# A linear-attention and MoE kernel: one 128-partition fetch per quad of chunks, in the order chunk, batch, head

## The chip, the cores and the metric

The kernel runs on one core of a Trainium2 chip. The metric is device time in microseconds of one launch; lower is better. Three runs of the kernel before gave 773.69, 776.86 and 777.75 us, so its time is the median, 776.86 us.

## The reference

An RWKV-7 style recurrence over 768 time steps, for 4 batches and 8 heads of dimension 40, is followed by an MLP over the 3072 tokens that it gives. All data is float32.

```python
for t in range(S):                                  # S = 768; B, H, D = 4, 8, 40
    y[:, :, t] = einsum('bhd,bhde->bhe', r_t, state)
    Sa = einsum('bhde,bhe->bhd', state, a_t)
    state = state * w_t[:, :, None, :] - einsum('bhd,bhe->bhde', Sa, b_t)
    state = state + einsum('bhd,bhe->bhde', v_t, k_t)
x = y.transpose(0, 2, 1, 3).reshape(B * S, H * D)   # 3072 x 320
h = x @ w_in                                        # w_in 320 x 2048
out = (h * cos(h)) @ w_out                          # w_out 2048 x 320
```

## The kernel before

Time is cut into 24 chunks of C = 32 steps. Inside a chunk the recurrence is turned into small matrix products, with all 4 batches and 8 heads at once: 128 partitions are 4 batches times 32 steps, or 64 partitions are one head's 40 features with padding. W, the running product of the decays w inside a chunk, scales a, b, k and the state. From chunk to chunk the state is handed on by the steps `t`, `q`, `x`, `s`, `z` of a chunk (`ch_t` to `ch_z`). In `ch_z` VectorE writes `qz`, GpSimd multiplies it by W (line 910) and makes `yt` (line 921), and `tokens` (line 926, SyncE's queue) stores it. Two chunks make a group; the MLP of a group (`fa`, `fb`, `y`, `sd` or `u`, `m`, `ms`, `c`) fills TensorE between the small products.

Everything is issued in an order that is written out by hand, the string `PLAN`: 1536 tokens such as `rf:r:2`. Each token calls one function, and each engine, and each DMA queue, takes its instructions in that order. Nothing is reordered at run time; an instruction that waits holds up all behind it on its engine. `B:n`, `K:n` and `P:n` are idle matmuls that keep TensorE busy.

The operands come in two ways. For early chunks they are loaded in natural layout (`load`, token `ld`, line 267) and transposed on TensorE. From the third quad of chunks on (a, r and v from quad 2, w from quad 3; a quad is four chunks; the dictionary `SINCE`) they are transposed through DRAM:

1. `rf:n:q` calls `quad_fetch` (line 278; for w `sf:q` calls it through `ws_fetch`): it loads one quad of one input into `ws`, 128 partitions of 32 steps x 40 features, 5120 B per partition. There is one `ws`. The partitions are (chunk, head, batch), which takes four DMAs of 32 partitions (line 282), each with the heads outermost.
2. `pt:n:q:i` (`quad_turn`, line 296, GpSimd) copies a third of the features out of `ws`, transposed in the free dimension, into one of two staging tiles `nat_a`; `st` (`quad_store`, line 303) stores it to DRAM as feature, partition, step. For w, `sc` (`ws_scan`, lines 350 and 355, VectorE) first makes W in `ws`, and `ss` stores it as the tensor `wd`.
3. `lt:c:n` (`turned_load`, line 323) loads one chunk of it with the features on the partitions, in two DMAs of 40 partitions: into `aT`, `rT`, `vp` (which holds v turned) or `wb` (W turned).
4. For chunks 12 to 23 `ld:c:w` also loads W in natural layout from `wd`, in one DMA (line 259), for `over_w` (token `r`, a reciprocal on VectorE).

The fetch of one quad cannot start before the last `pt` of the quad fetched before it has read `ws`.

Of the kernel before, what the change touches and what calls it, by code (L numbers as in the profile page):

```python
# [9 lines left out]
F32 = mybir.dt.float32  # L10
I32 = mybir.dt.int32
U32 = mybir.dt.uint32
ALU = mybir.AluOpType
# [7 lines left out]
sc:1 pb:2 lo:0 pn:2 lo:2 L:0:k:s:r is:0 ip:0:15 wf:1 wt:1 ip:0:14 ip:0:13 ip:0:12 ip:0:11 ip:0:10 ip:0:9  # L21
L:0:k:s:l L:0:v:p:l kn:0 k:0 wf:0 L:1:k:p:l ld:5:a ip:0:8 ip:0:7 in:0 L:1:v:s:l B:3 v:0 g:0 L:1:k:s:r wm:1
ip:0:6 ip:0:5 L:1:r:p:l wg:1 B:4 L:1:v:p:r kn:1 k:1 ip:0:4 wp:1 L:1:r:s:r in:1 v:1 wf:2 L:2:k:p:r ip:0:3 wt:2
ip:0:2 ip:0:1 ss:1 L:2:k:p:l x:0 it:0 g:1 B:4 L:2:v:s:r L:2:r:p:r ih:0 F:0:0:0 L:2:v:s:l ld:4:w wm:2 wf:3
S:0:0:0 wf:6 wg:2 wp:2 L:2:r:s:l wt:0 wg:0 s:0 wm:0 B:4 K:6 wt:3 wm:3 K:4 wf:4 wg:3 in:2 z:0 kn:2 B:5 t:1 q:1
wf:7 wp:0 ld:5:w L:3:r:p:l B:4 wp:3 F:0:1:0 K:14 wt:4 L:3:r:p:r wt:6 wm:4 F:0:2:0 L:3:v:p:l k:2 wg:4 wp:4
S:0:1:0 wf:8 wf:9 B:5 wf:5 K:6 L:3:v:s:r wt:7 wm:7 wg:7 wm:6 L:3:k:s:r wg:6 wp:6 x:1 wt:9 B:3 B:4 wp:7 s:1
wm:9 v:2 wg:9 wt:8 wm:8 B:4 wp:9 tk:0 wg:8 g:2 B:3 wf:10 wf:12 wt:5 wp:8 L:3:k:s:l wf:11 wt:10 wm:10 B:6 z:1
B:6 t:2 q:2 wg:10 ld:4:b B:6 wm:5 wg:5 tk:1 wp:5 in:3 wt:11 wm:11 B:3 wf:13 wp:10 x:2 kn:3 k:3 wt:13 tb:0 tb:1
wg:11 wp:11 S:0:2:0 v:3 ld:4:r wt:12 wm:13 wg:13 wp:13 wm:12 K:6 ld:4:k fa:0:0 fb:0:0 y:0:0:0 wg:12 wf:14  # L30
y:0:0:1 wt:14 wm:14 y:0:0:2 K:29 wg:14 g:3 s:2 wp:12 fa:0:1 ld:4:v fb:0:1 wp:14 F:0:3:1 y:0:1:1 y:0:1:0
sd:0:0:0 wf:15 wt:15 wm:15 wf:16 z:2 y:0:1:2 in:4 r:4 sd:0:0:1 sd:0:1:1 K:13 wt:16 wm:16 wf:17 S:0:3:1 wg:15
t:3 ld:5:b r:5 pw:4 wg:16 wp:15 K:20 ld:4:a sf:2 sc:2 q:3 ld:5:r fa:0:2 fb:0:2 y:0:2:0 x:3 pb:4 wt:17 ld:6:b
wm:17 y:0:2:1 wf:18 ld:7:w y:0:2:2 wp:16 sd:0:1:0 wf:19 wt:19 wm:19 kn:4 wg:17 wp:17 sd:0:2:1 ld:6:w ld:7:b
s:3 T:0:0 wg:19 pa:4 wt:18 wp:19 ss:2 r:6 ld:5:v ld:6:a pw:6 rf:a:2 r:7 tk:2 fa:0:3 pn:4 lo:4 fb:0:3 y:0:3:0
z:3 pb:6 ld:7:a pa:6 wg:18 pn:6 lo:6 y:0:3:1 y:0:3:2 wm:18 wp:18 is:4 ld:5:k sd:0:2:0 t:4 sp:4 ip:4:15 ld:8:w
kn:5 ld:8:b k:4 v:4 ip:4:14 g:4 ip:4:13 ip:4:12 ip:4:11 sd:0:3:0 in:5 tk:3 pt:a:2:0 ip:4:10 ip:4:9 ip:4:8
ip:4:7 ld:9:w tb:2 tb:3 ip:4:6 ip:4:5 v:5 k:5 fa:1:0 ip:4:4 ip:4:3 ip:4:2 st:a:2:0 q:4 g:5 fb:1:0 y:1:0:0
pt:a:2:1 ip:4:1 st:a:2:1 pt:a:2:2 st:a:2:2 rf:r:2 pt:r:2:1 ld:6:r lt:9:a x:4 pt:r:2:0 y:1:0:1 it:4 ld:9:b
ld:6:v sd:0:3:1 F:4:0:1 y:1:0:2 sd:1:0:0 ih:4 S:4:0:1 in:6 F:4:1:1 ld:6:k r:9 r:8 s:4 ld:11:b fa:1:1 pw:8  # L40
fb:1:1 y:1:1:0 z:4 lt:8:a y:1:1:1 sd:1:0:1 S:4:1:1 sp:8 T:1:0 F:4:3:1 F:4:2:1 t:5 pb:8 xa:9 xa:8 o:0:0
st:r:2:0 pt:r:2:2 ld:11:w y:1:1:2 fa:1:2 tk:4 ld:10:w rf:v:2 q:5 r:11 ld:10:b fb:1:2 x:5 sd:1:1:1 r:10 y:1:2:0
pn:8 sd:1:1:0 st:r:2:1 y:1:2:1 lt:11:a s:5 st:r:2:2 kn:6 ld:7:k ld:7:v pt:v:2:0 tb:4 v:6 y:1:2:2 sd:1:2:1 z:5
fa:1:3 k:6 pw:10 g:6 xa:11 st:v:2:0 fb:1:3 lt:10:a y:1:3:1 pb:10 S:4:3:1 tk:5 S:4:2:1 o:0:1 sd:1:2:0 y:1:3:0
# [84 lines left out]
def kernel(  # L129
# [145 lines left out]
    def re_laid(n, q):  # L275
        return q >= SINCE[n]
# [942 lines left out]
```

## Time and profile before

| | us |
|---|---|
| median of three runs | 776.86 |
| the profiled execution | 781.72 |
| its span, first to last instruction | 780.0 |
| TensorE busy in it | 714.6 |
| VectorE, ScalarE, GpSimd busy | 548.6, 358.3, 287.3 |
| busy share of the 16 DMA engines, 0 to 145 us / 145 to 560 / 560 to 780 | 0.62 / 0.54 / 0.18 |

Names of lines in the profile are those of the listing above. `SPq` is the queue of SyncE, which issues nearly all DMAs; `POOLq` is GpSimd's. The span from about 145 to 560 us is the one in which quads are fetched and turned; ahead of it lies the opening, in which the weights and the first chunks are loaded, and behind it the end, in which nothing more is fetched by quads.

### The profile page before, as it was taken

The page shows a single profiled execution, that of the slowest core. Times are in us where ns is not written, and L with a number is a line of the kernel's source. Part 1 is how long each engine was busy: PE and PEld are TensorE (multiplying, and loading weights), DVE is VectorE, ACT ScalarE, POOL GpSimd, SP SyncE. Part 2 cuts the span into 40 slices and gives each one's busy share as a digit, 9 for nine tenths or more (in the row PEclk, how much of TensorE's full clock was granted, in tenths as well). Part 3 has the DMA queues.
Part 4 walks back from the last instruction along what each step waited for, and adds up shares of the span by engine and source line. Part 5 has one row for each costly group of instructions (what it writes and reads, how often), then busy time and mean ns, then how long its engine had stood idle before and what let it go on. Part 6 is the DMA issues. An engine that isn't in the chain of part 4 may idle for free.

```text
span 780.0 us, 40147 instructions
## 1 busy us (share of the span) xinstructions
PE 714.6 (92%) x17948; PEld 588.9 (75%) x17948; DVE 548.6 (70%) x1199; ACT 358.3 (46%) x719; POOL 287.3 (37%) x466
## 2 busy tenths in 40 slices
PE   4758999899997989989899999899999999999996
PEld 3536678687785767878788778778888878888885
DVE  6988779887546886658878577899547886454343
ACT  1335574744544534543533544335445445445342
POOL 7624304233440562561452533542533223231111
PEclk9879999999999999999999999999999999999999
DMA  7675464554544456455446647447422231120100
GB/s 109 147 207 120 136 162 123 123 97 99 119 96 120 88 124 148 110 112 125 97 105 142 142 111 156 93 108 144 107 55 48 48 83 29 33 53 22 29 18 17
DMA packets 233405, 78.12 MB, mean 100 GB/s; under 512 B 193744, under 2 KB 224208, under 8 KB 233232
## 3 DMA queue, kind: packets, MB, share of 16 engines
q1 hardware_dynamic: 230992, 73.90, 42.4%
q8 instruction: 141, 2.31, 1.3%
q0 software_dynamic: 1152, 1.48, 1.0%
q10 hardware_dynamic: 1088, 0.16, 0.1%
q14 instruction: 32, 0.26, 0.1%
HBM read 54.53 MB, written 20.97 MB: 97 GB/s over the span
## 4 chain that ended last, share of the span: by engine, by line
PE 70%; DVE 9%; SPq 5%; DMA 5%; issue 4%; ACT 3%; POOL 2%; DVEq 0%; POOLq 0%; ACTq 0%
PE ph L210 25%; PE po L210 18%; PE dps L210 4%; PE x0ps L210 4%; PE gram L210 3%; PE sps L210 3%; PE p L210 2%; PE qps L210 2%; PE nps L210 2%; SPq L267 2%; PE sT L800 2%; DVE inv L652 1%; PE busy L210 1%; DMA xT<-xd 1%; ACT turns L995 1%
## 5 line engine op out<-in xcount | busy, mean ns | idle before, releaser
L210 PE MATMUL ph<-xT,w_in_sb 128*128 128x256 f32 x768 | 185.6, 388 | 5.3 <-DVE gT L998 2.4
L210 PEld LDWEIGHTS ph<-xT,w_in_sb 128*128 128x128 f32 x768 | 141.2, 191 | 34.0 <-issue 12.5
L210 PE MATMUL po<-w_out_sb,gT 128*128 128x160 f32 (+1 forms) x624 | 132.9, 353 | 0.9 <-DVE gT L998 0.8
L988 ACT ACTIVATE turns<-ph,few 128x512 f32<-128x512 f32 x96 | 63.6, 687 | 136.8 <-PE ph L210 134.6
L990 DVE SCALAR_TENSOR_TENSOR turns<-turns,ph 128x512 f32<-128x512 f32 x96 | 63.4, 684 | 84.8 <-ACT turns L988 84.2
L210 PEld LDWEIGHTS po<-w_out_sb,gT 128*128 128x128 f32 x624 | 99.8, 195 | 18.3 <-DVE gT L998 1.6
L910 POOL TENSOR_TENSOR qz<-qz,wc 128x160 f32<-128x160 f32 x92 | 40.2, 461 | 125.7 <-DVE qz L909 125.7
L998 DVE TENSOR_TENSOR gT<-ph,turns 128x512 f32<-128x512 f32 x96 | 65.1, 684 | 19.6 <-ACT turns L995 19.4
L296 POOL COPY nat_a<-ws 128x416 f32<-128x416 f32 (+1 forms) x45 | 46.5, 1044 | 70.0 <-DMA wdv<-nat_a 27.9
L995 ACT ACTIVATE turns<-turns,few 128x512 f32<-128x512 f32 x96 | 69.3, 722 | 3.1
L994 ACT ACTIVATE turns<-turns 128x512 f32<-128x512 f32 x96 | 59.9, 624 | 16.7 <-DVE turns L990 16.7
L1078 POOL TENSOR_TENSOR s<-gT 128x256 f32<-128x256 f32 x36 | 28.6, 795 | 82.8 <-DVE gT L1074 82.8
L652 DVE TENSOR_TENSOR inv<-inv,inv_tmp 128x31 f32<-128x31 f32 (+15 forms) x124 | 56.0, 452 | 4.3
L210 PE MATMUL ph<-xT,w_in_tail 64*128 64x256 f32 (+1 forms) x456 | 54.2, 396 | 0.0
L210 PE MATMUL po<-TW,gT 128*128 128x160 f32 x288 | 53.1, 308 | 0.1
L648 DVE TENSOR_TENSOR inv_tmp<-u,inv 128x31 f32<-128x31 f32 (+15 forms) x124 | 50.2, 405 | 2.7
L818 ACT COPY qz<-qps 40x256 f32<-40x256 f32 x92 | 33.8, 367 | 36.8 <-PE qps L210 35.4
L210 PEld LDWEIGHTS po<-TW,gT 128*128 128x128 f32 x288 | 45.1, 198 | 0.3 <-DVE gT L1074 0.3
L559 POOL TENSOR_TENSOR bn<-nat_b,rw 128x320 f32<-128x320 f32 x22 | 19.9, 908 | 67.6 <-DVE rw L558 51.7
L558 DVE RECIPROCAL rw<-nat_w 128x320 f32<-128x320 f32 x20 | 42.6, 2138 | 2.4 <-DMA nat_w<-wd 2.4
L1070 POOL TENSOR_TENSOR s<-gT 128x256 f32<-128x256 f32 x36 | 27.0, 751 | 46.6 <-DVE gT L998 29.0
L210 PEld LDWEIGHTS ph<-xT,w_in_tail 64*128 64x128 f32 (+1 forms) x456 | 32.2, 169 | 11.2 <-issue 6.6
(156 smaller groups left out, 1255.8 us busy)
## 6 DMA issues: line engine op xcount, KB each, us to landing
words<-in_moe_w_in_dram SPq DMA_DIRECT2D x8, 512.0 KB
xd<-yt SPq DMA_DIRECT2D x48, 80.0 KB
out_dram<-ot SPq DMA_DIRECT2D x24, 160.0 KB
nat_k<-in_k_dram SPq DMA_DIRECT2D x90, 40.0 KB
nat_v<-in_v_dram SPq DMA_DIRECT2D x88, 40.0 KB
nat_b<-in_b_dram SPq DMA_DIRECT2D x84, 40.0 KB
wd<-ws SPq DMA_DIRECT2D x5, 640.0 KB
xT<-xd SPq DMA_DIRECT2D x24, 128.0 KB
```

Of the source, the lines that this page charges most:

```text
L210: nc.tensor.matmul(o, lhsT=lhsT, rhs=rhs, start=start, stop=stop, skip_group_check=True)
L296: nc.gpsimd.tensor_copy(quad_part(n, q, i).rearrange("p (d t) -> p d t", t=C), ws[:, :, PARTS[i]].rearrange("p t d -> p d t"))
L558: nc.vector.reciprocal(rw, wn)
L648: nc.vector.tensor_tensor(tmp, u[:, j : j + 1, :j].to_broadcast([P, C - j, j]), x[:, j:, j : j + 1].to_broadcast([P, C - j, j]), ALU.mult,)
L652: nc.vector.tensor_tensor(x[:, j:, :j], x[:, j:, :j], tmp, ALU.subtract)
L818: nc.scalar.copy(pick(qz[rows], f * (NZ - C), (NZ, 2 * B), (1, C)), ps[f][rows, : 2 * B * C].rearrange("p (i t) -> p i t", t=C),)
L910: nc.gpsimd.tensor_tensor(z, z, wc.rearrange("p (f m b) -> p f m b", f=2, m=2)[:, :, :, bb] .unsqueeze(3).to_broadcast([P, 2, 2, D]), ALU. ...
L988: nc.scalar.activation(t, u, ACTF.Identity, bias=rnd, scale=1.0)
L990: nc.vector.scalar_tensor_tensor(t, t, -ROUND, u, ALU.add, ALU.subtract)
L994: nc.scalar.activation(t, t, ACTF.Abs)
L995: nc.scalar.activation(t, t, ACTF.Sin, bias=half_pi, scale=-2.0 * math.pi)
L998: nc.vector.tensor_tensor(gT[:, 2 * e : 2 * e + 2, :n], phs[e], ns[e].rearrange("p (f t) -> p f t", f=2), ALU.mult)
```

## The change

The partitions of `ws` become (chunk, batch, head). Batch and head lie behind one another in DRAM with one step, so one DMA of 128 partitions fetches the quad, with the chunks outermost (4 chunks, 32 pairs of batch and head, 5120 B). What follows from the new order of the partitions:

- `wd` is (chunk, batch, head, step, feature); natural W is loaded by four DMAs of 32 partitions instead of one of 128.
- In `turned_load`, r and v come back in runs of 512 B instead of 2048 B, a and W in runs of 128 B instead of 512 B.
- The turned tiles are laid out batch, head instead of head, batch. The matmuls take the same blocks of 32 columns from other places (`piece`); three elementwise operations (`turned_a`, the multiplication of `qz`, that of `yt`) walk W or their own tile in another order (`in_order`), with the same number of elements.

`PLAN` is another written order of the same steps: the tokens are the same, 1536 in number, but for the queues on which some first loads are issued (`L:chunk:input:queue:half`, queue s, a or p for SyncE, ScalarE, GpSimd, halves l and r of the four batches). The tokens from a fetch to the first that reads it (`pt`, or `sc` for w) are these:

| fetch | a2 | r2 | v2 | w3 | a3 | r3 | v3 | w4 | a4 | r4 | v4 | w5 | a5 | r5 | v5 |
|---|---|---|---|---|---|---|---|---|---|---|---|---|---|---|---|
| before | 38 | 1 | 19 | 1 | 12 | 16 | 12 | 9 | 31 | 1 | 14 | 24 | 13 | 15 | 31 |
| after | 12 | 5 | 21 | 4 | 1 | 7 | 11 | 10 | 10 | 5 | 1 | 2 | 19 | 3 | 1 |

The first lines of the written order, and the code:

```diff
@@ PLAN @@
 PLAN = """
-L:1:b:p:r L:0:a:s:l B:5 L:2:b:s:r L:1:a:p:r L:1:w:s:l L:0:v:p:r L:0:w:a:r L:0:w:s:l L:3:a:s:l B:4 L:3:b:p:l
-L:0:b:s:r L:1:w:a:r L:0:a:p:r L:2:w:s:r L:0:b:p:l L:1:a:s:l L:1:b:s:l L:2:w:s:l L:0:r:s:l L:3:b:s:r L:3:w:p:l
-L:3:w:s:r pw:0 L:2:a:s:l L:2:a:s:r L:2:b:s:l B:3 pa:0 L:0:r:p:r pw:2 L:3:a:s:r pa:2 pb:0 sp:0 pn:0 sf:1 B:2
...
+L:1:a:p:l L:2:w:s:l L:0:w:a:r L:0:b:p:r L:1:b:s:r L:0:v:p:r B:4 L:0:a:p:r B:5 B:3 L:3:w:s:r L:1:w:s:l
+L:1:w:a:r L:0:w:s:l L:3:b:p:r L:2:b:s:r L:3:w:s:l L:0:a:s:l L:0:k:s:r L:3:a:s:r L:1:a:p:r L:0:b:p:l L:2:b:s:l
+pw:0 L:2:w:s:r L:2:a:p:r L:0:r:s:r L:1:b:s:l L:2:a:p:l pa:0 L:3:b:p:l pw:2 L:3:a:s:l pa:2 sp:0 sf:1 pb:0 pn:0
+L:0:k:s:l sc:1 pb:2 pn:2 lo:2 L:0:v:s:l B:4 lo:0 kn:0 is:0 wf:1 L:0:r:s:l in:0 L:1:r:p:l L:1:k:p:r L:1:k:s:l
...
@@ -255,15 +255,10 @@
     def load(c, names, via=nc.sync, parts=range(B)):
         for n in names:
-            if n == "w" and re_laid("w", c // 4):
-                via.dma_start(
-                    nat[n, c][:, :, :D], wd[c // 4][c % 4].rearrange("h b t d -> (b t) h d")
-                )
-                continue
             for i in parts:
                 at_c = src[n][i, :, c * C : (c + 1) * C, :]
                 if n == "w" and c >= 4:
-                    at_c = wd[c // 4][c % 4, :, i] if re_laid("w", c // 4) else wd[c // 4][i, :, c % 4]
+                    at_c = wd[c // 4][c % 4, i] if re_laid("w", c // 4) else wd[c // 4][i, :, c % 4]
                 via.dma_start(nat[n, c][blk[i], :, :D], at_c.rearrange("h t d -> t h d"))
@@ -277,12 +272,11 @@
     def quad_fetch(n, q):
-        for i in range(4):
-            x = src[n]
-            nc.sync.dma_start(
-                ws[blk[i]].rearrange("p t d -> p (t d)"),
-                bass.AP(x.tensor, x.offset + (4 * q + i) * C * D, [[S * D, H], [H * S * D, B], [1, C * D]]),
-            )
+        x = src[n]
+        nc.sync.dma_start(
+            ws.rearrange("p t d -> p (t d)"),
+            bass.AP(x.tensor, x.offset + 4 * q * C * D, [[C * D, 4], [S * D, B * H], [1, C * D]]),
+        )
     PARTS = [slice(0, 14), slice(14, 27), slice(27, D)]
@@ -319,20 +313,32 @@
             G[tag, c] = aT_b[c % 6] if n == "a" else sb2.tile([P, 4, P], F32, tag=tag, name=tag)
             to = G[tag, c].rearrange("p j t -> p (j t)")
         for e in range(2):
-            x = turned_d[n, c // 4][:, 4 * H * (c % 4) : 4 * H * (c % 4 + 1)]
-            nc.sync.dma_start(
-                to[half[e]].rearrange("p (j t) -> p j t", j=4),
-                x.rearrange("d (f j b) t -> f d j (b t)" if n in "vr" else "d (j f b) t -> f d j (b t)", f=2, b=B)[e],
-            )
+            x = turned_d[n, c // 4][:, B * H * (c % 4) : B * H * (c % 4 + 1)]
+            if n in "vr":
+                at_e, x = to[half[e]].rearrange("p (b n) -> p b n", b=B), x.rearrange("d (b f j) t -> f d b (j t)", f=2, b=B)
+            else:
+                at_e, x = to[half[e]].rearrange("p (n t) -> p n t", t=C), x.rearrange("d (n f) t -> f d n t", f=2)
+            nc.sync.dma_start(at_e, x[e])
     def turned_w(c):
         wc = G["wc", c] = ring.tile([P, 4 * B], F32, tag="wc", name="wc")
         nc.gpsimd.tensor_copy(wc, G["wb", c][:, C::C])
         from_one(c)
+    def in_order(n, c, x):
+
+        form = "p (b j) t -> p j b t" if re_laid(n, c // 4) else "p (j b) t -> p j b t"
+        return x.rearrange(form, j=4)
+
+    def piece(n, c, rows, j, b):
+
+        if re_laid(n, c // 4):
+            return G[n + "T", c][rows, b, j * C : (j + 1) * C]
+        return G[n + "T", c][rows, j, blk[b]]
+
     def turned_a(c):
-        aT = G["aT", c].rearrange("p j t -> p (j t)")
-        nc.vector.tensor_tensor(b4(aT), b4(aT), G["wx", c], ALU.mult)
+        aT = in_order("a", c, b4(G["aT", c].rearrange("p j t -> p (j t)")))
+        nc.vector.tensor_tensor(aT, aT, in_order("w", c, G["wx", c]), ALU.mult)
     def ws_fetch(q, via=nc.sync):
         if re_laid("w", q):
@@ -356,7 +362,7 @@
             n //= 2
     def ws_store(q):
-        wd[q] = dram.tile([4, H, B, C, D] if re_laid("w", q) else [B, H, 4, C, D], F32, tag="wd", name="wd")
+        wd[q] = dram.tile([4, B, H, C, D] if re_laid("w", q) else [B, H, 4, C, D], F32, tag="wd", name="wd")
         nc.sync.dma_start(wd[q].rearrange("x y z t d -> (x y z) (t d)"), ws.rearrange("p t d -> p (t d)"))
     def first_load(c, name, queue, parts):
@@ -606,7 +612,7 @@
                     for e in range(2):
                         mm(
                             ps[e][blk[bb ^ e], (4 * i + j) * C : (4 * i + j + 1) * C],
-                            G["bT", c + i][half[e], j, blk[bb]], G["aT", c + i][half[e], j, blk[bb]],
+                            G["bT", c + i][half[e], j, blk[bb]], piece("a", c + i, half[e], j, bb),
                             i == 0 and j == 0,
                         )
@@ -750,21 +756,21 @@
         nc.scalar.copy(G["kT", c].rearrange("p j t -> p (j t)"), ps)
     def p2_g(c):
-        kT, vT, aT, rT = G["kT", c], G["vT", c], G["aT", c], G["rT", c]
+        kT = G["kT", c]
         ps = two("gram")
         for j in range(4):
             for bb in range(B):
                 for e in range(2):
                     mm(
                         ps[e][blk[bb], j * C : (j + 1) * C], kT[half[e], j, blk[bb]],
-                        aT[half[e], j, blk[bb]], j == 0,
+                        piece("a", c, half[e], j, bb), j == 0,
                     )
         for j in range(4):
             for bb in range(B):
                 for e in range(2):
                     mm(
-                        ps[e][blk[bb], (4 + j) * C : (5 + j) * C], vT[half[e], j, blk[bb]],
-                        rT[half[e], j, blk[bb]], False,
+                        ps[e][blk[bb], (4 + j) * C : (5 + j) * C], piece("v", c, half[e], j, bb),
+                        piece("r", c, half[e], j, bb), False,
                     )
         ag = sb2.tile([P, H, C], F32, tag="ag", name="ag")
         n = HH * C
@@ -811,7 +817,7 @@
                 for f in range(2):
                     mm(
                         ps[f][half[e], i * C : (i + 1) * C], G["s", c][half[f], i, half[e]],
-                        G["rT", c][half[f], 2 * (i % 2) + e, blk[i // 2]], i == 0,
+                        piece("r", c, half[f], 2 * (i % 2) + e, i // 2), i == 0,
                     )
         for f in range(2):
             for rows in half:
@@ -837,7 +843,7 @@
                     for e in range(2):
                         mm(
                             ps[e][blk[bb ^ e], j * N72 : (j + 1) * N72],
-                            G["aT", c][half[e], j, blk[bb]], qz[half[e], bb, j % 2, o : o + N72], False,
+                            piece("a", c, half[e], j, bb), qz[half[e], bb, j % 2, o : o + N72], False,
                         )
         x0 = [sb1.tile([P, 4 * N72], F32, tag=f"x0{e}", name=f"x0{e}") for e in range(2)]
         nc.scalar.copy(x0[0], ps[0][:, : 4 * N72])
@@ -909,7 +915,9 @@
                 nc.vector.tensor_tensor(z, pick(dp, 0, (2 * N72 + C, 2), (N72, 2), (1, D)), z, ALU.add)
                 nc.gpsimd.tensor_tensor(
                     z, z,
-                    wc.rearrange("p (f m b) -> p f m b", f=2, m=2)[:, :, :, bb]
+                    wc.rearrange(
+                        "p (b f m) -> p f m b" if re_laid("w", c // 4) else "p (f m b) -> p f m b", f=2, m=2
+                    )[:, :, :, bb]
                     .unsqueeze(3).to_broadcast([P, 2, 2, D]),
                     ALU.mult,
                 )
@@ -918,9 +926,12 @@
                 pick(dp, D, (2 * N72 - D, 2), (N72, 2), (1, C)),
                 pick(qz[:, bb], 0, (NZ - C, 2), (NZ, 2), (1, C)), ALU.add,
             )
-        nc.gpsimd.tensor_tensor(
-            yt.rearrange("p j b t -> p (j b) t"), yt.rearrange("p j b t -> p (j b) t"), wx, ALU.mult
-        )
+        if re_laid("w", c // 4):
+            nc.gpsimd.tensor_tensor(yt, yt, in_order("w", c, wx), ALU.mult)
+        else:
+            nc.gpsimd.tensor_tensor(
+                yt.rearrange("p j b t -> p (j b) t"), yt.rearrange("p j b t -> p (j b) t"), wx, ALU.mult
+            )
         G["yt", c] = yt
     def tokens(c):
```

More of the change, by code (lines that the diff above doesn't have):

```diff
@@ new lines @@
+ld:6:r F:4:2:1 t:5 fa:1:2 tk:4 lt:10:a S:4:1:1 q:5 ld:10:b fb:1:2 xa:9 in:6 y:1:2:0 ld:7:k x:5 lt:11:a
+sd:1:1:0 s:5 k:6 pt:v:2:0 r:11 sp:8 y:1:2:1 sd:1:1:1 pt:v:2:1 pn:8 y:1:2:2 sd:1:2:1 z:5 o:0:0 ld:7:v tk:5
+fa:1:3 v:6 pw:10 xa:10 st:v:2:0 pt:v:2:2 tb:4 g:6 r:10 fb:1:3 ld:7:r in:7 y:1:3:0 y:1:3:1 S:4:3:1 xa:11
+sd:1:2:0 tb:5 pb:10 S:4:2:1 y:1:3:2 o:0:1 pn:10 is:8 sf:3 t:6 ij:8:31 fa:2:0 sc:3 kn:7 k:7 q:6 v:7 ij:8:30
+st:v:2:2 fb:2:0 y:2:0:1 x:6 sd:1:3:0 sd:1:3:1 ij:8:29 ij:8:28 ij:8:27 ij:8:26 st:v:2:1 ss:3 y:2:0:0 lt:8:r
@@ new lines @@
+ld:12:b y:2:0:2 ij:8:25 ld:12:w ld:13:w s:6 pt:w:3:0 st:w:3:0 lt:8:v fa:2:1 fb:2:1 z:6 y:2:1:1 ij:8:24
+sd:2:0:0 sd:2:0:1 T:0:1 y:2:1:0 y:2:1:2 T:3:0 o:1:0 r:12 tk:6 g:7 ld:8:v ld:8:k ij:8:23 ij:8:22 t:7 fa:2:2
+ij:8:21 q:7 o:1:1 pt:w:3:2 fb:2:2 x:7 T:0:2 T:0:3 y:2:2:1 lt:9:r pt:w:3:1 st:w:3:2 ij:8:20 ij:8:19 y:2:2:0
+kn:8 y:2:2:2 sd:2:1:0 k:8 st:w:3:1 s:7 ld:9:k sd:2:1:1 ij:8:18 ij:8:17 ij:8:16 z:7 ij:8:15 ij:8:14 rf:a:3
+pt:a:3:1 pt:a:3:0 ld:13:b ld:9:v kn:9 lt:12:w fa:2:3 r:13 fb:2:3 sd:2:2:1 T:1:1 g:8 tk:7 ij:8:13 y:2:3:1
@@ new lines @@
+m:3:1:0 fa:3:2 fb:3:2 ld:14:b x:9 rf:v:3 y:3:2:0 o:2:0 lt:10:v u:3:1:2 m:3:1:1 tk:8 xa:12 T:3:1 lt:13:a
+ld:14:w pt:v:3:0 lt:11:r xa:13 u:3:1:3 y:3:2:1 sp:12 s:9 lt:14:w y:3:2:2 lt:15:a T:3:2 ld:11:k r:15 o:2:1
+u:3:2:0 pn:12 T:3:3 k:10 xw:14 fa:3:3 st:v:3:0 T:2:3 z:9 tb:8 r:14 pt:v:3:1 pt:v:3:2 fb:3:3 y:3:3:0 t:10
+lt:14:a xa:14 tk:9 m:3:2:0 u:3:2:1 y:3:3:1 u:3:2:2 g:10 y:3:3:2 lt:15:w xw:15 xa:15 m:3:2:1 u:3:2:3 pb:14
+pn:14 u:3:3:0 u:3:3:1 m:3:3:0 u:3:3:2 is:12 sf:4 ij:12:31 ij:12:30 tb:9 ij:12:29 ij:12:28 st:v:3:1 m:3:3:1
@@ new lines @@
+tk:13 fa:5:3 st:v:4:1 r:18 fb:5:3 m:5:2:0 u:5:2:2 g:14 u:5:2:3 pt:v:4:2 y:5:3:1 m:5:2:1 y:5:3:0 xa:18 pb:18
+y:5:3:2 lt:19:w t:14 xw:19 xa:19 pn:18 u:5:3:0 u:5:3:1 tb:13 is:16 sf:5 fa:6:0 sc:5 q:14 m:5:3:0 ij:16:31
+ij:16:30 ij:16:29 ld:15:v fb:6:0 x:14 pt:w:5:1 ld:15:k st:v:4:2 u:5:3:2 kn:15 k:15 y:6:0:1 m:5:3:1 u:5:3:3
+ms:5 c:5:0 y:6:0:0 ij:16:28 ss:5 c:5:1 ij:16:27 u:6:0:0 ij:16:26 ld:20:b y:6:0:2 u:6:0:1 pt:w:5:0 fa:6:1
+ld:21:b c:5:3 c:5:2 lt:15:v st:w:5:0 pt:w:5:2 s:14 ld:16:k st:w:5:1 ij:16:25 ij:16:24 fb:6:1 y:6:1:0 rf:a:5
@@ new lines @@
+z:14 m:6:0:0 u:6:0:2 t:15 y:6:1:2 y:6:1:1 ld:20:w u:6:0:3 ij:16:23 st:w:5:2 g:15 lt:16:v m:6:0:1 u:6:1:0
+ld:16:v u:6:1:1 ij:16:22 ij:16:21 pt:a:5:1 fa:6:2 q:15 o:5:0 pt:a:5:0 st:a:5:0 r:20 o:5:1 fb:6:2 y:6:2:1
+lt:17:r m:6:1:0 lt:16:r x:15 u:6:1:2 ld:21:w tk:14 ij:16:20 y:6:2:0 y:6:2:2 kn:16 ld:17:v k:16 s:15 ld:17:k
+ij:16:19 ij:16:18 ij:16:17 ij:16:16 pt:a:5:2 m:6:1:1 u:6:1:3 st:a:5:2 ij:16:15 ij:16:14 z:15 fa:6:3 fb:6:3
+y:6:3:0 u:6:2:0 u:6:2:1 m:6:2:0 u:6:2:2 ij:16:13 t:16 y:6:3:2 y:6:3:1 kn:17 g:16 m:6:2:1 ij:16:12 r:21 tb:14
@@ new lines @@
+ms:7 c:7:1 c:7:2 ij:20:31 lt:19:v st:v:5:2 s:18 o:7:0 u:8:0:0 ij:20:30 kn:19 k:19 ld:20:k ld:20:v ij:20:29
+ij:20:28 u:8:0:1 fa:8:1 ij:20:27 c:7:3 ij:20:26 ij:20:25 st:v:5:1 z:18 fb:8:1 g:19 kn:20 ij:20:24 m:8:0:0
+u:8:0:2 tk:18 ij:20:23 ij:20:22 t:19 q:19 m:8:0:1 u:8:0:3 y:8:1:1 y:8:1:0 ij:20:21 y:8:1:2 u:8:1:0 k:20 x:19
+u:8:1:1 m:8:1:0 u:8:1:2 lt:21:r lt:20:v lt:20:r ld:21:k fa:8:2 ij:20:20 u:8:1:3 ij:20:19 ij:20:18 ij:20:17
+ij:20:16 s:19 o:7:1 fb:8:2 z:19 y:8:2:0 tk:19 y:8:2:1 m:8:1:1 t:20 u:8:2:0 y:8:2:2 u:8:2:1 fa:8:3 q:20
@@ L119 @@
+u:11:2:1 fa:11:3 fb:11:3 y:11:3:0 m:11:2:0 u:11:2:2 u:11:2:3 y:11:3:1 m:11:2:1 y:11:3:2 u:11:3:0 u:11:3:1
+m:11:3:0 u:11:3:2 u:11:3:3 m:11:3:1 c:11:0 c:11:1 c:11:3 ms:11 c:11:2 o:11:0 o:11:1
 """
```

163 lines of the change are left out of this document (65 added, 98 removed).

## The prediction

> **What bounds the kernel now.** I read the page, then busy time by stage, then what each engine waited for, then the lines of `ws`. TensorE bounds it:
>
> ```profile
> PE 714.6 (92%) x17948; PEld 588.9 (75%) x17948; DVE 548.6 (70%) x1199; ACT 358.3 (46%) x719; POOL 287.3 (37%) x466
> PE 70%; DVE 9%; SPq 5%; DMA 5%; issue 4%; ACT 3%; POOL 2%; DVEq 0%; POOLq 0%; ACTq 0%
> ```
>
> The first line is busy time, the second the chain that ended last. Of 780.0 us TensorE is idle for 65. By stages its busy time is 115.8 of 145 us, 390.1 of 415 and 208.7 of 220, so 29, 25 and 11 us of idle. The fetches by quads lie in the middle stage. What TensorE waited for there (total, times, longest):
>
> ```profile
> PE gram L210 <- issue: 5.0, 4, 2.6
> PE nps L210 <- issue: 4.5, 4, 2.3
> PE sps L210 <- ACT x L843: 3.7, 1, 3.7
> PE ph L210 <- DVE gT L998: 2.4, 2, 1.8
> PE bT L514 <- DVE yt L916: 1.9, 1, 1.9
> ```
>
> About half is "issue", behind no other engine; the waits for engines that another order could take away are some 12 us, one of 3.7 the largest. So the upside is small, a few us. What happened at that largest one, and at three other fetches (in brackets the idle time ahead):
>
> ```profile
> 231.90 2.93 SPq L282 DMA_DIRECT2D ws<-in_w_dram  x4
> 239.14 1.35 DVE L350 TENSOR_TENSOR ws<-ws 128x640 f32<-128x640 f32 x2 [6.27 <-DMA ws<-in_w_dram]
> 247.02 0.31 PE L210 MATMUL sps<-x,rt 32*32 32x72 f32 x2 [3.69 <-ACT x L843]
> ...
> 180.72 1.98 POOL L296 COPY nat_a<-ws 128x416 f32<-128x416 f32 x2 [7.80 <-DMA aT<-wda]
> 301.71 1.99 POOL L296 COPY nat_a<-ws 128x416 f32<-128x416 f32 x2 [9.44 <-DMA aT<-wda]
> 422.11 1.98 POOL L296 COPY nat_a<-ws 128x448 f32<-128x448 f32 x2 [5.46 <-DMA nat_b<-in_b_dram]
> ```
>
> The fetch w3 is issued at 231.90 and read at 239.14, 7.24 us later; VectorE stands for 6.27 us and TensorE then loses 3.69. The GpSimd rows are the fetches r2, r3 and r4: each is issued 7.0 to 7.4 us before the copy begins, so it is the fetch that is waited for, whatever name stands behind the arrow. GpSimd is 37% busy and usually loses nothing by it.
>
> How fast a fetch is (us; busy of PE, PEld, DVE, ACT, POOL; clock; DMA share; GB/s):
>
> ```profile
> 118.00:120.64 2.64, 2.64 (x69) 1.99 (x52) 2.64 (x11) 1.59 (x3) 1.50 (x4) 1.00 0.82 254
> 233.42:238.58 5.16, 5.16 (x150) 4.19 (x152) 0.00 (x0) 3.81 (x8) 0.00 (x0) 1.00 0.42 133
> ...
> L282 SPq DMA_DIRECT2D ws<-in_w_dram x12: 665/686/752, 231.9 to 457.7; - x12
> L341 SPq DMA_DIRECT2D ws<-in_w_dram x2: 587/648/708, 18.1 to 116.6; - x2
> ```
>
> Both stretches hold one transfer of 655 KB in rows of 5120 B and next to nothing else. The first is L341, one DMA whose outermost count is 32; the second the four DMAs of L282, outermost count 8. The DMA time is the same, 0.82 x 16 x 2.64 = 34.6 us and 0.42 x 16 x 5.16 = 34.7, but the second has half of the engines, and takes twice as long.
>
> **The change part by part.**
>
> *SyncE's queue.* Removed: 60 issues of L282 at 0.67 us, 40.2. Added: 15 at 0.65 (L341, the nearest row), 9.8; W's natural load becomes four issues (L267, 0.45 us) instead of one (L259, 0.39) for 12 chunks, 21.6 - 4.7 = 16.9. Net -13.5 us of queue time. SPq is 5% of the chain, but mostly as waiting for producers; I take -1, between -4 and 0.
>
> *The landing of a fetch.* The new DMA has outermost count 4. Going from 32 to 8 halved the engines; the bounds are 34.7 us of DMA time over 16 engines (2.2 to 2.64 us as measured) and over 4 (8.7 us). With 1.5 us from issue to first packet (231.90 to 233.4) and 0.5 from the last packet to VectorE's start, it lands 4.6 or 10.7 us after its issue, where it was 7.24. I take 10.7, since L282 against L341 is a row for just this difference. The Trainium skill ("DMA: Bandwidth & Descriptors", in the section on why a DMA increments its semaphore by 16, paragraph "How many engines (k)") says that a DMA runs on the largest number up to 16 that divides the outermost sizes of both sides: 16, 8 and now 4. The trace agrees on 16 and 8; no run shows the 4 yet. By that rule the sum is the forecast's, by 16 engines that of the first rival below.
>
> *Who waits.* The new order puts the reader closer behind the fetch: the median distance falls from 14 tokens to 5, and distances of up to 5 tokens go from 3 of 15 to 8. Before, five fetches were waited for: 7.80, 6.27, 9.44, 5.46 and 1.77 us (v3), 30.7 in all, and TensorE lost 4.2 us at w3 (3.69 and 0.49 right behind), 1.0 at r2 (0.49 and 0.54, the latter for GpSimd's memset of `half` queued behind the copy), and nothing I can attribute at the others: 5.2 / 30.7 = 0.17 us per us waited. After: 8 close ones at 8 us (10.7 less what SyncE runs ahead) and three of 7 to 10 tokens (r3, w4, a4) at 3 us, 73 in all, 42 more. At 0.17 that is +7 us. The bounds: 0, if all are like r4 (nothing lost), and 42 x 4.2 / 6.27 = +28, if all are like w3. Queued behind a waiting `pt` on GpSimd are `qz` and `yt` of `ch_z`, `kn`, `bn` and the sums `s`; behind a waiting `sc` on VectorE the cosine's and the chain's steps. Loads issued behind the fetch stand behind it on the engines that it holds and land up to 3 us later; I count that in the same term.
>
> *Shorter runs.* `aT` and `wb` come in 56 DMAs of 640 runs instead of 160, the same bytes (80 KB). `wda<-nat_a` and its like already write runs of 128 B, so the size is nothing new here. They are prefetched; the worst waits for them now are 16.8 us of GpSimd in 5 times (`wc`), not of TensorE. I take +0.5, between 0 and 3, the four W loads included (VectorE waited 2.4 us once for one).
>
> *Elementwise walks.* The `yt` product takes 1.27 us for 128x512 (2.5 ns an element), the `qz` product, which already walks strided and broadcast operands, 0.44 us for 160 (2.7): no change of rate to be expected, 0. The matmuls keep shapes and number: 0. If the walk cost a tenth more on 12 chunks it would be 0.13 us each, on an engine with 63% idle.
>
> *The opening.* The first wait is for `a` of chunk 0:
>
> ```profile
> 9.97 1.15 POOL L267 DMA_DIRECT2D nat_a<-in_a_dram x2
> 14.44 0.63 PE L514 MATMUL aps<-ident,nat_a 128*128 128x128 f32 x4 [2.65 <-DMA nat_a<-in_a_dram]
> ```
>
> Those loads move from the fifth place on GpSimd's queue to the fourth, 1.15 us earlier; `a` of chunk 1 goes from the second to the sixth, where it lands at about 15.4, just when it is read now (15.43). VectorE's inverse of quad 0 loses one weight step (`wp:1`, 0.6 us) from ahead of it. I take -1, between -2 and +1. GpSimd now issues a2 between `pw:0` and `pa:0`, at about 14 to 16 us; read at 20.4, it is in time.
>
> *The end* is the same work in the same order on TensorE; 0. The rest of the order: 0, between -4 and +4, since the movable idle time of the middle is 12 us.
>
> The sum against the profiled execution: 781.7 - 1 + 7 + 0.5 - 1 = 787.2. The median of the runs stands 4.9 lower (776.86 to 781.72), so 782.3, +0.7%. A measurement of this kernel tells some 0.5% (3.9 us) from no change.
>
> **The rivals.**
>
> *Faster: the fetch gets all 16 engines, like L341.* It lands after 4.6 us instead of 7.24. For it: 128 partitions on the other side, as in L341. Against it: outermost count 4. Eleven waits of about 3 us are 33 us, as many as now, but w3's 3.69 us of TensorE shrinks by 2.6; with the queue's -1 to -2 and the opening's -1 that is -5: 772. It decides if a fetch takes under 5 us. The Trainium skill (same page, "Rules for kernel authors") advises 128 partitions and few large transfers; by that rule alone this rival would be the forecast. The same time comes out if the fetch is slow but SyncE issues it well ahead.
>
> *No difference.* GpSimd has 63% of its time free, and r3 and r4 cost TensorE nothing; if all the new waits are like these, 777.
>
> *Much slower.* GpSimd's waits fall ahead of `qz` in most quads, and the state's chain loses as at w3: +28 - 2, about 803.
>
> **How the numbers follow.** Forecast (781 to 795) 0.48; much slower 0.10; no difference 0.15; faster 0.27, since an order with less idle time is possible for reasons I cannot see in parts. Slower by over 0.5% is 0.58. The range 767 to 798 takes in the faster case with the order's -4 and most of the slower ones.
>
> **What would show it.** Right: in the stretch of a fetch the DMA share near 0.25 and 8 us or more of 5120 B rows; 15 issues of the fetch, near 0.65 us each; waits of `nat_a` copies on GpSimd well over the 70.0 us of now; TensorE idle in 145 to 560 us over 25. Wrong: a fetch of 2.6 us at a share near 0.8; or long fetches whose readers do not wait, because SyncE is ahead; or a difference that arises before 145 or after 560 us, where no quad is fetched.

## The result: 44 us slower, and the profile after

The kernel after takes 819.0 us (median of 4 runs, 816.0 to 826.6), the kernel before 775.3 in the same comparison: a ratio of 1.060 (95% interval 1.049 to 1.070). Slower by 5 us was forecast, in a range that ended at 798 us, and it is slower by 44. Ratios, here and below, leave out runs that lie over 1.5% above the fastest of their kernel; medians are of all runs. The profiled execution took 817.4 us, its span is 815.7. Busy time, and the chain of work that ended last:

```profile
PE 725.2 (89%) x17948; PEld 593.8 (73%) x17948; DVE 551.4 (68%) x1199; ACT 360.5 (44%) x719; POOL 289.9 (36%) x468
PE 47%; DVE 21%; DMA 12%; POOL 6%; SPq 6%; issue 4%; ACT 4%; DVEq 0%; POOLq 0%; ACTq 0%
```

TensorE's instructions are as many, but its share of the chain fell from 70% to 47%. TensorE is idle for 90.5 us (65.4 before), and the same matmuls take 10.6 us longer. So the 35.7 us by which the two profiled spans differ are 25.1 of idle time and 10.6 of busy time (they differ by less than the medians, since the profiled execution before was one of the longer ones). The stage in which quads are fetched (us, busy of PE, PEld, DVE, ACT, POOL, clock, DMA share, GB/s):

```profile
145.00:560.00 415.00, 370.52 (x9573) 302.24 (x9574) 283.54 (x610) 179.74 (x365) 160.97 (x239) 0.95 0.52 105
```

9573 matmuls ran in these 415 us, where it had been 10439, and TensorE is idle for 44 of them instead of 25. The `yt` product of chunk 3 starts 1.6 us earlier than before, that of chunk 5 8.4 later, of chunk 8 14.8, 11 21.2, 14 36.3; from there to chunk 23 it stays between 33 and 37. The loss arises where quads are fetched, and nowhere else. What TensorE waited for there (total, times, longest):

```profile
PE nps L210 <- DVE aT L341: 8.5, 2, 5.2
PE bT L520 <- POOL bn L565: 6.3, 2, 4.4
PE kT L520 <- POOL kn L740: 5.3, 2, 2.8
...
PE ph L210 <- DMA xT<-xd: 2.8, 1, 2.8
```

No large wait carries it: there are some twenty waits of at most 5.2 us, spread over all operands. The fetch itself, from what uses `ws` (least/median/longest issue in ns; then who waited for `ws`, in us and times):

```profile
L276 SPq DMA_DIRECT2D ws<-in_w_dram x3: 582/606/917, 238.0 to 491.2; - x3
...
  POOL nat_a L290: 70.8, 8
  DVE ws L356: 12.4, 3
```

Each fetch is one issue of about 0.6 us, as predicted. GpSimd's copies waited for `ws` eight times, 70.8 us in all: six times for a fetch (43.0 us) and twice for VectorE's scan of w (27.7 us). The fetch w3, which opened the prediction, in the timeline (idle time ahead in brackets):

```profile
238.04 0.58 SPq L276 DMA_DIRECT2D ws<-in_w_dram  x1
249.80 2.22 DVE L356 TENSOR_TENSOR ws<-ws 128x640 f32<-128x640 f32 x5 [6.62 <-DMA ws<-in_w_dram]
253.87 1.05 POOL L290 COPY nat_a<-ws 128x448 f32<-128x448 f32 x1 [14.95 <-DVE ws L361]
```

From issue to reader it is 11.8 us now, where it was 7.24. Rows of 5120 B stand in the trace for 7.4 to 10.7 us per fetch. Where the fetch has the engines to itself, they are busy to 0.26, about 4 of 16 (clock, DMA share and GB/s at the end):

```profile
246.00:247.00 1.00, 1.00 (x8) 0.92 (x7) 0.00 (x0) 0.94 (x4) 0.00 (x0) 1.00 0.26 108
```

At r2, r3, r4 and a5 the copy waited for one thing more. It writes a staging tile whose last store is issued 0.7 to 3.0 us behind the fetch, and by the trace's semaphores that store landed 1.0 to 1.7 us after the fetch did. At r2:

```profile
181.02 0.99 POOL L290 COPY nat_a<-ws 128x416 f32<-128x416 f32 x1 [11.44 <-DMA wda<-nat_a]
```

What the prediction had not looked for is in SyncE's queue. Behind a fetch the *issues* themselves last long. A fetch of r, and one of v, with what is issued behind:

```profile
169.61 0.60 SPq L276 DMA_DIRECT2D ws<-in_r_dram  x1
170.25 6.38 SPq L297 DMA_DIRECT2D wda<-nat_a  x2
...
205.36 0.58 SPq L276 DMA_DIRECT2D ws<-in_v_dram  x1
...
206.50 11.88 SPq L262 DMA_DIRECT2D nat_r<-in_r_dram  x4
```

Two issues take 6.38 us and four take 11.88, where one has a median of 0.45. All issues of three kinds (least/median/longest, ns):

```profile
L297 SPq DMA_DIRECT2D wda<-nat_a x12: 382/471/5860, 165.1 to 552.0; - x12
L262 SPq DMA_DIRECT2D nat_v<-in_v_dram x88: 311/450/8304, 17.9 to 718.4; - x88
L942 SPq DMA_DIRECT2D xd<-yt x48: 273/358/4932, 78.5 to 762.1; - x48
```

The medians are nearly those of before (491, 450 and 357 ns), but the longest had been 1324, 2222 and 955. I call *held* what SyncE's rows of issues in 140 to 640 us last beyond 0.55 us per issue, summed over the rows in which it is over 1.5 us: 26 us before, 102 after. One such case through to TensorE:

```profile
332.76 0.60 SPq L276 DMA_DIRECT2D ws<-in_v_dram  x1
339.23 5.21 SPq L321 DMA_DIRECT2D aT<-wda  x2
343.12 1.05 POOL L290 COPY nat_a<-ws 128x448 f32<-128x448 f32 x1 [6.01 <-DMA ws<-in_v_dram]
347.16 0.69 DVE L341 TENSOR_TENSOR aT<-aT,wb 128x512 f32<-128x512 f32 x1 [4.23 <-DMA aT<-wda]
347.91 0.76 PE L210 MATMUL nps<-aT,bT 40*32 40x32 f32 x64 [3.22 <-DVE aT L341]
```

The second load of `aT` is held in its issue until 344.4, VectorE waits 4.23 us for it, TensorE 3.22 for VectorE; no reader of `ws` stands between them. And then the clock (last column but two):

```profile
344.00:348.00 4.00, 0.78 (x81) 0.67 (x86) 0.84 (x2) 0.32 (x2) 2.83 (x6) 1.00 0.41 77
348.00:352.00 4.00, 3.76 (x74) 3.20 (x75) 3.51 (x5) 1.84 (x4) 0.41 (x1) 0.57 0.71 129
```

After those 3.22 us the granted clock is 0.57 for the next four, which is another 0.43 x 3.76 = 1.6 us lost, by this estimate. The longer busy time fits that: the mean clock of the middle stage fell from 0.98 to 0.95, and 0.03 x 370.5 is 11 us.

### The profile page after: what moved, and what is told of

It is laid out like the page before. It is cut to its first block, busy times and chain, and to the rows that moved or that the text cites. A ratio compares the mean times of both kernels' runs of the same rounds, so it can differ in the third digit from the quotient of the medians.

```text
span 815.7 us, 40129 instructions
## 1 busy us (share of the span) xinstructions
PE 725.2 (89%) x17948; PEld 593.8 (73%) x17948; DVE 551.4 (68%) x1199; ACT 360.5 (44%) x719; POOL 289.9 (36%) x468
## 4 chain that ended last, share of the span: by engine, by line
PE 47%; DVE 21%; DMA 12%; POOL 6%; SPq 6%; issue 4%; ACT 4%; DVEq 0%; POOLq 0%; ACTq 0%
PE ph L210 16%; PE po L210 11%; DVE inv L658 4%; DVE inv_tmp L654 3%; DMA ws<-in_a_dram 3%; PE x0ps L210 3%; DMA ws<-in_w_dram 3%; PE dps L210 3%; DMA xd<-yt 3%; PE p L210 2%; PE gram L210 2%; SPq L321 2%; DVE gT L1009 2%; PE sps L210 2%; DVE rw L564 2%
## 5 line engine op out<-in xcount | busy, mean ns | idle before, releaser
L210 PE MATMUL ph<-xT,w_in_sb 128*128 128x256 f32 x768 | 189.2, 393 | 5.6 <-DMA xT<-xd 3.5
L210 PEld LDWEIGHTS ph<-xT,w_in_sb 128*128 128x128 f32 x768 | 143.5, 195 | 35.6 <-issue 12.3
L1089 POOL TENSOR_TENSOR s<-gT 128x256 f32<-128x256 f32 x36 | 27.7, 769 | 81.7 <-DVE gT L1085 81.7
L654 DVE TENSOR_TENSOR inv_tmp<-u,inv 128x31 f32<-128x31 f32 (+15 forms) x124 | 52.3, 422 | 2.4
L915 DVE TENSOR_TENSOR qz<-dps,qz 128x160 f32<-128x160 f32 x92 | 29.1, 316 | 14.0 <-PE dps L210 13.7
```

Source lines behind the costliest of these rows:

```text
L210: nc.tensor.matmul(o, lhsT=lhsT, rhs=rhs, start=start, stop=stop, skip_group_check=True)
L654: nc.vector.tensor_tensor(tmp, u[:, j : j + 1, :j].to_broadcast([P, C - j, j]), x[:, j:, j : j + 1].to_broadcast([P, C - j, j]), ALU.mult,)
```

## The experiments

Times of a comparison stand beside the kernel before on the same chip (772.6, 773.9, 772.5 and 772.5 us in the four of them); ratios are with their 95% intervals. Kernels 5 to 10 have two runs each, the others three or more. What was expected of each stands ahead of its result; there e1 is kernel 1, and so on.

**Which part of the change.** Kernels 1 and 4 fetch with four DMAs, each with 32 outermost, in the new order of partitions; 1 has the new written order, 4 that of before. Kernel 2 is the new code in the old order, 3 the old code in the new order.

```diff
     def quad_fetch(n, q):
         x = src[n]
-        nc.sync.dma_start(
-            ws.rearrange("p t d -> p (t d)"),
-            bass.AP(x.tensor, x.offset + 4 * q * C * D, [[C * D, 4], [S * D, B * H], [1, C * D]]),
-        )
+        for i in range(4):
+            nc.sync.dma_start(
+                ws[blk[i]].rearrange("p t d -> p (t d)"),
+                bass.AP(x.tensor, x.offset + (4 * q + i) * C * D, [[S * D, B * H], [1, C * D]]),
+            )
```

Kernel 1: 

> The changed kernel and its written order, with one edit: each quad is fetched by four DMAs of 32 partitions, one per chunk, whose outermost count is 32 (batch and head) instead of one DMA with outermost count 4. Engines theory (the fetch holds 4 of 16 engines and takes 8 to 10.7 us; that is the loss): a fetch now takes 2.6 to 4 us and the time falls to 770 to 785 us. Order theory (the written order is worse whatever the fetch takes): it stays at 810 to 825. Short-runs theory (a and W in runs of 128 B, W's load in four pieces): also 810 to 825.

Kernel 2: 

> The changed kernel's functions, slow fetch included, with the written order of the kernel before. Engines theory: the fetch is as slow as in the changed kernel, but the readers stand a median of 14 tokens behind it instead of 5, so part of the loss goes: 785 to 810 us. Order theory: 772 to 782. Short-runs theory: 810 to 825.

Kernel 3: 

> The functions of the kernel before (four fetch DMAs on 8 engines, landing 7.2 us after issue) with the new written order. Engines theory: the order stands its readers too close even for 7.2 us, a part of the loss: 785 to 805 us. Order theory: 810 to 825. Short-runs theory: 772 to 782.

Kernel 4: 

> The fetch of e1 (four DMAs of 32 partitions, outermost count 32) with the rest of the changed code and the written order of the kernel before. Engines theory: 768 to 780 us, since the fetch is now faster than that of the kernel before, whose order left room for a slower one. Order theory: 772 to 782. Short-runs theory: over 790.

Measured: kernel 1 771.8 us (0.995, 0.990 to 1.000), kernel 2 826.0 (1.069, 1.062 to 1.076), kernel 3 772.3 (0.997, 0.992 to 1.002), kernel 4 768.5 (0.996, 0.991 to 1.001). So the loss goes with the fetch as one DMA with 4 outermost, and nothing of it that shows with the written order, the runs of 128 B or the four loads of W, which kernel 1 has all of. Two expectations missed: the longer distance of the old order gave the slow fetch no relief (826, not 785 to 810), and the new order costs nothing beside 8 engines (772, not 785 to 805). Who waits for `ws` in kernel 4:

```profile
  POOL nat_a L291: 27.7, 7
  DVE ws L357: 2.3, 1
```

That is 30.0 us of waiting, where kernel 2, which differs in the fetch alone, has 65.3 (the copies that wait for the scan of w, 6.0 and 2.5 us, are in both sums). The sixty issues are back, of 0.42 us each.

Kernel 1 again, with more rounds: 

> e1 once more with more rounds: the changed kernel and its order with the fetch as four DMAs of 32 partitions. Measured 0.9948 of the kernel before (0.9900 to 0.9996). Engines theory: 0.990 to 1.000; the short runs, the four loads of W and the new order cost nothing that shows.

It took 770.7 us (0.998, 0.994 to 1.002; span 765.9, held 15 us): level with the kernel before. No version beat that one clearly.

**Are the late readers the cause, or the other transfers?** Kernel 5 is kernel 4 with an unread copy of 655 KB from DRAM to DRAM behind each fetch, 4 outermost; 10 and 6 are the same with 8 and 32 outermost. Nothing reads the copy, and the fetch that the readers of `ws` wait for is the fast one.

```diff
+        spare = dram.tile([P, C * D + D], F32, tag="unread", name="unread")
+        nc.sync.dma_start(spare[:, : C * D], bass.AP(x.tensor, x.offset + 4 * q * C * D, [[C * D, 4], [S * D, B * H], [1, C * D]]))
```

Kernel 5: 

> e4 (four DMAs of 32 partitions on 16 engines, old written order) and, right behind each of the 15 fetches on SyncE's queue, one more DMA that copies the same 655 KB from DRAM to DRAM with outermost count 4; nothing reads what it writes, so this kernel does extra work that the reference does not ask for. Queue theory (what costs is that all loads issued behind a 4-engine transfer stand behind it on those engines): 800 to 830 us, although the fetch itself is as fast as in e4. Reader theory (what costs is that the readers of ws wait for the fetch): 766 to 780.

Kernel 6: 

> As e5, but the copy that nobody reads walks batch and head outermost (count 32), the same bytes in the same rows. Control for the bytes alone: both theories 768 to 782 us, the transfer lasting 2 to 4 us on 16 engines. If it comes out at 800 or more, the extra bytes and not the number of engines cost in e5.

Kernel 10: 

> As e5 (e4 and a copy of 655 KB behind each fetch that nobody reads, extra work), with the copy's outermost count 8 instead of 4; its rows are other ones of the same input, 5120 B each. A dose between e6 (16 engines, 785 us, profiled run 779) and e5 (4 engines, 828). Shared-engines theory: the most loaded engines are full for some 6.5 us per fetch instead of 10.8 (e5) and 4.3 (e6): 788 to 808 us. If any number under 16 costs the same, 820 or more; if only 4 does, under 785.

Measured: 828.5 us on 4 engines (1.072, 1.059 to 1.085), 800.1 on 8 (1.039, 1.032 to 1.045), 784.6 on 16 (1.015, 0.995 to 1.036), against 768.5 without. The same bytes cost 60, 32 and 16 us, of which the 16 are not clear of noise (the interval of kernel 6 takes in 1). 5 and 10 came as the theory of the queues had it, 6 a little above. What uses `ws` in kernel 5 waits no more for it than in kernel 4 (four waits of `nat_a` for a fetch, 21.9 us, and one of VectorE, 6.4, against 30.0 in all), so the loss needs no late fetch. GpSimd is later all the same, by another way: its copies wait 48.1 us for the stores that free their staging tiles, where it was 18.9 in kernel 4. Issues are as long as in the kernel after:

```profile
L945 SPq DMA_DIRECT2D xd<-yt x48: 273/357/6571, 71.6 to 771.5; - x48
```

**Another queue for the fetch.** Kernels 7 and 8 are kernel 2 with the fetch issued by `nc.gpsimd` or `nc.scalar` instead of `nc.sync`.

Kernel 7: 

> The changed code with the old written order (e2, 826 us), the one fetch DMA issued from GpSimd's queue instead of SyncE's, so that it does not stand in the same line as the other loads. If the trace shows it on 4 engines (8 to 11 us): queue theory 775 to 795, reader theory 815 to 830. If the trace shows it on 16 engines (2.6 to 4 us) it tells nothing apart, and both theories say 768 to 782.

Kernel 8: 

> As e7, from ScalarE's queue. ScalarE must wait there until the last turn of the quad before has run, which may cost some us of its own at up to 15 places. Queue theory: 778 to 800 us, with the fetch on 4 engines lasting 8 to 11 us or more; reader theory: 815 to 840.

Measured: 828.4 us (1.072, 1.059 to 1.085) and 848.4 (1.098, 1.084 to 1.111). In kernel 7 the packets of a fetch still come 4 to 6 at a time and take 8 to 11 us, and the issues that SyncE makes of *other* transfers are as long as in the kernel after:

```profile
L297 SPq DMA_DIRECT2D wda<-nat_a x12: 359/472/6261, 167.0 to 552.3; - x12
```

SyncE is held (86 us) by a fetch that it did not issue, so it is the four engines that count and not the queue. The time is the one that the theory of the readers gave, but the trace takes the reason away: the other transfers were not spared. The Trainium skill ("DMA: Bandwidth & Descriptors", section "Issuing engines are not separate DMA queues") says that whatever queue starts a DMA, it runs on the same 16 engines; these held issues agree with it. In kernel 8 ScalarE stands as well (idle for 10.61 us around the issue of r3), and it is slower still.

**Late readers alone.** Kernel 9 is kernel 4 (fast fetch, no further DMA), with 46 small memsets of 0.11 us on GpSimd ahead of a quad's first copy and 84 of 72 ns on VectorE ahead of W's scan: some 80 us of busy time in all.

```diff
+        if n != "w" and (n, q) not in begun:
+            begun.add((n, q))
+            for _ in range(46):
+                nc.gpsimd.memset(idle_sb, 0.0)
...
+        if q >= 3:
+            for _ in range(84):
+                nc.vector.memset(idle_dv, 0.0)
```

> e4 (fetch on 16 engines, old written order) with the engine that first reads each fetched quad held for about 6 us just before it reads: 46 small memsets on GpSimd before the first turn, 84 on VectorE before the scan of w. That is what a 4-engine fetch adds for its reader (5 to 6 us after issue becomes 11 to 12), in the worst case, since it is added even where the reader came late; no DMA is changed. Shared-engines theory (the loss comes from all the other transfers that are slowed while 4 engines are full): 768 to 790 us. Reader theory (the held engine holds up the chain): 800 to 830.

It took 823.1 us (1.069, 1.062 to 1.075), SyncE held 16 us. TensorE's waits in it, of the middle:

```profile
PE sps L210 <- DVE x L863: 12.0, 2, 11.6
PE sps L210 <- ACT x L862: 9.2, 1, 9.2
PE kT L533 <- POOL kn L753: 7.5, 2, 5.6
```

That is the number of the theory of the readers: late readers alone would do it too, 54.6 us over kernel 4 for 80 us of memsets, or 0.68 us per us. The memsets hold their engine at all 15 places, also where the reader was not late in the changed kernel.

**SyncE held alone.** Kernel 12 is kernel 4 with twelve unread copies of 512 B behind each fetch, 16 outermost.

```diff
+        spare = dram.tile([12, 16, 8], F32, tag="unread", name="unread")
+        for i in range(12):
+            nc.sync.dma_start(spare[i], bass.AP(x.tensor, x.offset + i * C * D, [[S * D, 16], [1, 8]]))
```

> The kernel of the run with 32 outermost in the order of before (768.5), and behind each of the 15 fetches twelve copies of 512 B from DRAM to DRAM that nobody reads, 16 outermost, on SyncE's queue: 180 issues of about 0.4 us, 72 us of issue time in all, about 5 us behind each fetch, and next to no time of the DMA engines. In the changed kernel SyncE's issues right behind a fetch last up to 8.3 us instead of 2.2; what rows of SyncE last beyond 0.5 us an issue, where that is over 1.5 us, comes to 88 us in 140 to 640 us (20 before; 28, 39, 61 and 97 in the runs with 32 outermost and with the unread copy on 16, 8 and 4 engines, which took 768, 785, 800 and 828). Theory of the held queue: a fetch on 4 engines costs because SyncE is held in the issues behind it, so holding SyncE alone by as much gives 805 to 830. Rival, the transfers themselves: they are slow on the full engines and SyncE's hold is hidden; 766 to 778, and 778 to 805 where both matter.

(Counted over whole rows and beyond 0.55 us per issue, as above, the sums of held time in that text are 102 for the kernel after and 26, 28, 45, 56 and 103 for the others.) It took 861.6 us (1.112, 1.104 to 1.121). An issue was longer than expected:

```profile
L283 SPq DMA_DIRECT2D unread<-in_r_dram x48: 506/589/1651, 176.8 to 591.0; - x48
```

A group of twelve lasts 8.1 to 11.0 us with the gaps, the fifteen groups 133 us together. The chain that ended last in this kernel:

```profile
PE 40%; SPq 32%; DMA 9%; DVE 6%; issue 5%; POOL 4%; ACT 4%; DVEq 0%; POOLq 0%; ACTq 0%
```

SyncE has taken 32% of it (6% in the kernel after). The time grew by 93 us over kernel 4's: 0.70 us per us that SyncE is held, beyond the range given because it was held for 133 us and not 72; the rival, 766 to 778, falls. By the count of the table below (133 us and 18 of held issues of other transfers, less kernel 4's 28) it would be 0.76. Side by side:

| kernel | fetch on / unread copy on | SyncE held, us | own issues of the copy, us | time, us |
|---|---|---|---|---|
| 4 | 16 / none | 28 | 0 | 768.5 |
| 1, again | 16 / none | 15 | 0 | 770.7 |
| 6 | 16 / 16 | 45 | 10 | 784.6 |
| 10 | 16 / 8 | 56 | 12 | 800.1 |
| 5 | 16 / 4 | 103 | 10 | 828.5 |
| after | 4 / none | 102 | 0 | 819.0 |
| 2 | 4 / none | 117 | 0 | 826.0 |

At 0.70, kernels 6, 10 and 5 should lose 19, 28 and 60 us against kernel 4 (held time and own issues less 28); they lose 16, 32 and 60. The kernel after is held 87 us longer than kernel 1 and issues its fetches in 10 us instead of 37; the difference, 60, gives 42 us, and it loses 48. Kernel 2 against kernel 4 likewise: 89 less 23, 46 us, and it loses 57. In the last two kernels of the table the readers are late at the same places, so the table cannot say which of the two the time goes with there.

## Why the prediction was wrong

Right were: that a fetch with 4 outermost runs on a quarter of the engines; the issue (0.60 us, 0.65 forecast); the landing, nearly (11.7 us from issue to a reader that waited, on the average of 14 waits; 10.7 forecast); that GpSimd's idle time ahead of its copies would be well over 70 us (143); that the opening loses nothing (the `yt` products of chunks 0 to 3 come between 1.6 us earlier and 2.5 later, which cannot tell the forecast -1 from 0), nor the end (between chunks 14 and 23 the lag moves by 3 us or less) and the order, the short runs and the elementwise walks at next to nothing (kernels 1 and 3). The Trainium skill's rule of the largest divisor up to 16 of the outermost sizes ("DMA: Bandwidth & Descriptors", section on why a DMA increments its semaphore by 16) now has its third row here: 16, 8 and about 4 engines with 2.64, 5.16 and 7.4 to 10.7 us for the same 655 KB. Of the rivals, "faster" falls with it, and so does "no difference". "Much slower" priced the waits at 0.67 us per us; with the waiting that was measured (below) it would have come to 817 instead of 803. That this is so near to 819 is in part luck, since it lays the whole loss on the readers and has nothing for SyncE's issues or the clock.

The step that failed is *Who waits*, and in it the price, 0.17 us of TensorE per us waited. Waits of first readers behind a fetch grew from 31 to 94 us where 73 was forecast (94 with those that the profile puts down to other DMAs, as the 11.44 us above): a smaller error. But 63 us more of waiting came with 44 us more of time, 0.70 per us if all of it is laid on the waits, which is near the bound that the text set aside (4.2 / 6.27 = 0.67 at w3) and four times the mean over five waits. Three things went wrong in it:

1. It counted only TensorE's idle time directly behind a wait. In a written order where each engine takes its instructions in turn, a late GpSimd or SyncE comes out some steps later, under another name: of the waits listed above none names `ws`. Kernels 9 and 12 hold engines by a known time, and both give 0.7.
2. It let the transfers queued behind the fetch ride "in the same term". They are a cost of their own, which kernel 5 shows without a late fetch, and kernel 12 shows a way that suffices: SyncE is held. The term for SyncE's queue, -13.5 us of issues and -1 in the sum, had the wrong sign: in 140 to 640 us SyncE's issues last some 425 us instead of 360, although the fetches' own fell from 44 to 10.
3. It left out the clock: 10.6 of the 35.7 us of span are matmuls that run slower, where the granted clock is lower after idle stretches.

The distances in tokens, the reason for so many new waits, did not matter either: kernel 2 has the longer ones and is no faster.

What stays open is how the 44 us divide between held issues and late readers in the changed kernel itself. Each alone suffices, both fall into the same 10 us behind a fetch, and they do not add: kernel 2, which has both, loses no more than kernel 5, which has the one. Kernels 7 and 8 lose more than SyncE's held time gives: 86 and 91 us, less the 28 of kernel 4 and the 32 of its fetches' issues, which left SyncE, times 0.70 is 18 and 22 us, and they lose 60 and 80. So the readers, or the engine that now issues, count in them.

The chain that ended last leans to the readers. In the kernel after it runs through four fetches, a2, w3, a4 and w5, from issue to landing (start and length in us):

```profile
148.41 11.41 DMA ws<-in_a_dram
238.04 11.67 DMA ws<-in_w_dram
402.81 13.02 DMA ws<-in_a_dram
491.23 11.29 DMA ws<-in_w_dram
```

That is 47 us, where one fetch with 4.8 us was on it before, and SyncE's share of the chain is 6% where it was 5%. In kernel 5, whose loss needs no late fetch, SyncE has 19%, and fetches 3 us:

```profile
PE 48%; SPq 19%; DMA 12%; DVE 8%; POOL 5%; issue 4%; ACT 4%; DVEq 0%; POOLq 0%; ACTq 0%
```

A chain is one path of one execution, and the other transfers on it can hold a held issue, so it does not divide the 44 us; but it shows late fetches on the path.

## What to carry to other kernels

Put a multiple of 16 outermost in a DMA (in these runs it was the DRAM side that varied), even if that takes four issues instead of one: 128 partitions did not make the transfer wide, the outermost count did. A transfer on few engines can cost as much by what it does to the others (kernel 5) as late readers do (kernel 9): look for long issues on the queue behind it, not only for its own reader. In a tight in-order schedule, price lateness near the worst ratio that the trace shows, here 0.7 us per us in kernels 9 and 12, and not by the idle time that the few present waits happen to cause.

## What the runs showed of the hardware

- While a transfer on about 4 engines is under way, an issue on SyncE's queue lasts up to 8.3 us instead of 0.45, also when that transfer came from another queue (6.26 us in kernel 7), and all issues behind it wait. That the issue waits for room on those engines is the likely reason; no run shows it.
- The tiny copies of kernel 12, 512 B, took 0.59 us each to issue, more than the 0.42 of a fetch of 164 KB.
- An idle time of 3.22 us was enough to bring TensorE's granted clock to 0.57 over the next 4 us; after 4.42 us at 231.5 it was 0.50 and 0.66 in 236 to 244 us. In the kernel before, 2.18 us that ended at 386.8 were followed by 0.50 from 387.5 to 390.5 us; in the kernel after, 2.84 us at 371 were not followed by a lower clock. The Trainium skill ("TensorE: Matmul & The Clock Gate", Part 1) has the clock halve after an idle window of about 3.4 us, until the array has been busy as long. The trace agrees on the half clock, but shorter idle times were enough here, though not always.
